# A two-layer decode kernel: one key/value head instead of two with stationary output weights, and an up projection with stationary weights

## The chip, the cores and the metric

The kernel runs on one core of one Trainium2 chip. The metric is the device time of one execution in microseconds (us), as the median of several runs. Lower is better. The profile is of one execution, taken by the hardware profiler.

## What is computed

One token for each of four requests passes twice through the same pair of blocks, attention with cached keys and values and then a gated feed-forward block:

```python
x = A_x
x = x + _A_ref(_layernorm(x), A_k_cache, A_v_cache, A_wq, A_wo)
x = x + _B_ref(_layernorm(x), B_w_gate, B_w_up, B_w_down)
x = x + _A_ref(_layernorm(x), A_k_cache, A_v_cache, A_wq, A_wo)
x = x + _B_ref(_layernorm(x), B_w_gate, B_w_up, B_w_down)

# _A_ref: q = x @ wq; softmax(q k^T / sqrt(128)) v over 4096 cached positions; @ wo
# _B_ref: (gelu(x @ w_gate) * (x @ w_up)) @ w_down
```

D is 512, there are 32 query heads and 8 key/value heads of 128, so that four query heads (rep) share a key/value head, and the feed-forward width is 1792. Keys and values of one request are 8 MB each; all of the cache is 67 MB in bfloat16.

## The kernel before

The kernel does not go block by block over all requests. For each request b it finishes the first attention and the first feed-forward block, and then uses the keys of that request that are still in SBUF for the second attention, while the keys of request b + 1 take their place. So the keys are read once, the values nearly twice (two tiles of a pass are kept).

**The stages.** `attend(None, 0)` (L495) is the first attention of request 0, with the loading of all weights. Then the loop at L662 runs over b = 0 to 3: `dense` (L643) finishes the first layer of request b for one row, queries for its second attention are built, and `attend(b, b + 1)` does the second attention of b and the first of b + 1 together. For b = 3 `attend_last` (L603) does the second attention alone. One more `dense` call for all four rows, and the output is written.

**Values in steps.** A key/value head of values comes in two tiles of 512 KB. `Values.step` (L466) does one such tile: 16 matmuls with a block of values as the stationary operand and four columns of probabilities as the moving one, into `ot`. A pass of one request over its values has 16 steps. Seven buffers hold value tiles; after a step the buffer is free and `load_v` (L453) issues the next load from the SP queue. After every four steps, which are two key/value heads, one VectorE instruction (L487) multiplies `ot` with the reciprocal of the softmax sum and writes eight columns of `OT_bf` (first attention) or `OT2_bf` (second). The last 14 steps of the second attention's pass are spread over the following dense stage and the start of the next `attend`: `fill` (L663) and `rest` are calls of its `step`. So between the matmuls of the dense stage there are value steps.

**The output projection.** `pairs` (L492) gives the first query head of each of the four groups of eight heads, in the order in which the values finish. Three groups go through `out_proj` (L275), "the rows": each head's column of `OT_bf` is stationary and the 512 columns of its `wo` rows move; the four heads of a key/value head go to four strips of 32 partitions of a PSUM tile `rows`. When the three groups are in, `y_rows` (L259) turns `rows` in 32x32 blocks on VectorE (L215) and copies it (L261), and `y_select` (L264) adds the four strips up with 8 small matmuls into `y`. The fourth group, which finishes last, goes through `out_proj_end` (L283): blocks of `wo` are stationary, 4 for each head, and a head's column moves. That adds into `y` and needs no turn. So 8 heads are 32 matmuls there.

**The dense stage** calls in this order: `out_proj_end`, fill(1), the addition to x (`add_y`, L290) and the layernorm sums, fill(1), the gate projection `ffn_in` (L300) with `wg_sb`, fill(1), the up projection with `wu_sb`, `gelu`, `gate_up`, fill(2), `down` (L344) and a second `add_y`. For one row (nb = 1) `ffn_in` keeps the row stationary and moves the weights, 64 matmuls of 448 columns, into `rows`; `ffn_cols` (L319) then turns the rows with one VectorE instruction. For four rows it keeps 128x128 weight blocks stationary and moves the rows, 56 matmuls, and no turn follows.

**Order.** The order of instructions on each engine is the order of the program. The places that matter below: in `attend`, L594 to L601, the last five value steps of the pass with the third group of heads, `y_rows` and `y_select` between them; in `attend_last`, L629 to L641, the same for four rows; in `attend`, L513 to L523, `rest(1)`, the second group's scores, `soft`, `rest(1)`, `soft_turn` (L408, a VectorE turn of `pp`, L410), `soft_swap`, `rest(2)`.

Of the kernel before, what the change touches and what calls it, by code (L numbers as in the profile page):

```python
# [30 lines left out]
def kernel(  # L31
# [240 lines left out]
    def head_rhs(o_bf, i):  # L272
        return o_bf[:, i:i + 1] if len(o_bf.shape) == 2 else o_bf[:, i, :]

    def out_proj(rows, o_bf, h0, hp, at):  # L275
        for n in range(hp):
            i = h0 + n
            lhsT = head_rhs(o_bf, i)
            r0 = (i % QD) * QS
            nc.tensor.matmul(rows[r0:r0 + lhsT.shape[-1], :], lhsT=lhsT, rhs=wo_sb[:, i, :],  # L280
                             start=(at == 0 and n < QD), stop=(at == 2 and n >= hp - QD))

    def out_proj_end(y, o_bf, h0, hp):  # L283
        for k in range(KD):
# [12 lines left out]
            nc.vector.tensor_tensor(out=XX[:, 0, bs], in0=XX[:, 0, bs],  # L297
                                    in1=y.rearrange("p k b -> p b k"), op=ALU.add)

    def ffn_in(b0, nb, w_sb):  # L300
        bs = slice(b0, b0 + nb)
        rows = new_rows()
        if nb > 1:
            h = rows[:, :KF * nb].rearrange("p (c j) -> p c j", j=nb)
            for c in range(KF):
                for k in range(KD):
                    nc.tensor.matmul(h[:, c], lhsT=w_sb[:, k, c * P:(c + 1) * P],
                                     rhs=xn_bf[:, k, bs], start=(c == 0 and k == 0),
                                     stop=(k == KD - 1), skip_group_check=True)
            return h  # L310
        for k in range(KD):
            w = w_sb[:, k].rearrange("p (n a i) -> p a n i", a=QD, i=QS)
            for j in range(QD):
                nc.tensor.matmul(rows[j * QS:j * QS + nb, :KF * QS], lhsT=xn_bf[:, k, bs],  # L314
                                 rhs=w[:, j], start=(k == 0), stop=(k == KD - 1))
        return rows

    def ffn_cols(h, nb):
        return h if nb > 1 else turn_rows(h, KF * QS)[:, :, :nb]  # L319

    def gelu(nb, rows, rstd):
        hg = ffn_cols(rows, nb)
# [139 lines left out]
    class Values:  # L462
# [3 lines left out]
        def step(self, count=1):  # L466
            for _ in range(count):
                use = self.order[self.n]
                assert order[seen["use"]] == use
                seen["use"] += 1  # L470
                b, last, g, s, t = use
                pe, rden = self.prob[g]
                if self.n % (2 * NT) == 0:
                    self.ot = ps_ot.tile([P, 2, rep], FP32, name="ot", tag="ot")
                self.n += 1
                load_v()
                v = held[b, g, s, t]
                for i in range(CH):
                    c = t * CH + i
                    nc.tensor.matmul(self.ot[:, s % 2], lhsT=v[:, i, :], rhs=pe[:, s, c, :],  # L480
                                     start=(c == 0), stop=(c == C - 1), skip_group_check=True)
                if last or (b, g, s, t) not in keep:
                    free.append(held.pop((b, g, s, t)))
                load_v()
                if self.n % (2 * NT) == 0:
                    s0 = s - s % 2
                    nc.vector.tensor_tensor(  # L487
                        out=self.dst(g * GH + s0).rearrange("p (k h) -> p k h", h=rep),
                        in0=self.ot[:], in1=rden[:, s0:s0 + 2], op=ALU.mult)


    def pairs(order):  # L492
        return [(order[n][2] * GH + order[n][3] // 2 * 2) * rep for n in range(0, VB, 2 * NT)]

    def attend(b2, b1, next_q=None, rest=None):  # L495
        two, first = b2 is not None, b1 == 0
# [1 line left out]
        ga, gb = groups(b1)  # L498
        keys = Keys(b1)
        turn = keys.turn  # L500
        vals = Values(b1, 0, prob1, lambda k: OT_bf[:, k * rep:(k + 2) * rep])
        vals2 = None
        if two:
            vals2 = Values(b2, 1, prob2, lambda k: OT2_bf[:, k * rep:(k + 2) * rep, b2])
            sc2 = [new_scores(i) for i in range(NG)]
            seen["hold"] = True
            scores(sc2[0], ga, 0)
            keys.load(GH)
            qm1 = next_q()
            scores(sc2[0], ga, 1)  # L510
            keys.load(GH)
            q_build(qm1, gb)
            rest(1)  # L513
            for t in range(NT):
                scores(sc2[1], gb, t)
                keys.load(GH)
            seen["hold"] = False
            load_v()
            p0 = soft(sc2[0])
            rest(1)  # L520
            soft_turn(p0)
            pe0, den0 = soft_swap(p0, p2p), soft_den(p0)
            rest(2)  # L523
            qm = q_spread(q1_bf[:, ga, :, b1], amask, ga)
            turn()
            prob2[ga] = (pe0, soft_recip(den0))
            q_build(qm, ga)
            vals2.step(KEEP)
            turn(3)
        else:  # L530
            load_wq(0)
            keys.load(TG)
            load_wq(1)
            keys.load(TG)
            load_v()
            make_identity(nc, ident_bf[:])
            build_consts()
            xT_ps = ps_sm.tile([P, KD, B], BF16, name="xT_ps", tag="sm")
            for k in range(KD):
                nc.tensor.transpose(xT_ps[:, k, :], x_bf[:B, k * P:(k + 1) * P], ident_bf[:B, :B])  # L540
            nc.vector.tensor_copy(out=XX[:, 0].rearrange("p b k -> p k b"), in_=xT_ps[:])
            ln_square(0, B)
            rstd1 = ln_rstd(B, ln_center(0, B))
            q_first(q_rows(0, B, 0), 0, rstd1)
            build_q1(0, 0)
            turn(4)
# [26 lines left out]
        soft_turn(p0)  # L573
        if not first:
            for i in range(2):
                out_proj(rows, OT_bf, heads[i], hp, i)
        pe, den = soft_swap(p0, p1p), soft_den(p0)
        if two:
            p1 = soft(sc2[1])
# [6 lines left out]
        if first:  # L586
# [2 lines left out]
            seen["upto"] = len(loads)  # L589
            load_v()  # L590
            for i in range(3):
                out_proj(rows, OT_bf, heads[i], hp, i)
            y = y_select(y_rows(rows, 1), 1)
        else:  # L594
            vals.step(2)
            out_proj(rows, OT_bf, heads[2], hp, 2)
            yc = y_rows(rows, 1)
            vals.step()
            y = y_select(yc, 1)
            vals.step(2)  # L600
        return (y, OT_bf, heads[3], hp), vals2  # L601

    def attend_last(b2, next_q, rest):  # L603
        prob2 = {}
        ga, gb = groups(b2 + 1)
        vals = Values(b2, 1, prob2, lambda k: OT2_bf[:, k * rep:(k + 2) * rep, b2])
        sc2 = [new_scores(i) for i in range(NG)]
        def freed(t):
            scores(sc2[0], ga, t)
# [19 lines left out]
        vals.step(4)  # L629
        soft_turn(p0)  # L630
        prob2[gb] = (soft_swap(p0, p2p), soft_recip(soft_den(p0)))
        out_proj(rows, OT2_bf, heads[0], hp, 0)
        vals.step(5)
        out_proj(rows, OT2_bf, heads[1], hp, 1)
        vals.step(4)
        out_proj(rows, OT2_bf, heads[2], hp, 2)
        yc = y_rows(rows, B)
        vals.step(2)
        y = y_select(yc, B)
        vals.step()  # L640
        return y, OT2_bf, heads[3], hp  # L641

    def dense(b0, nb, proj, fill):  # L643
        out_proj_end(*proj)
# [3 lines left out]
        ln_square(b0, nb)  # L648
        mv = ln_center(b0, nb)
        fill(1)  # L650
        rg = ffn_in(b0, nb, wg_sb)
        fill(1)
        ru = ffn_in(b0, nb, wu_sb)
        sq, h = gelu(nb, rg, ln_rstd(nb, mv))
        H_bf = gate_up(nb, sq, h, ru)
        fill(2)
# [71 lines left out]
```

## Time and profile before

| What | us |
|---|---|
| median of 7 runs | 314.33 |
| lowest and highest | 313.27 and 316.86 |
| the profiled execution, device time | 314.11 |
| its span, first to last instruction | 312.3 |
| TensorE matmuls (PE) busy | 211.7 (68%) |
| TensorE weight loads (PEld) busy, beside matmuls | 123.2 (39%) |
| VectorE (DVE) busy | 169.9 (54%) |
| ScalarE (ACT) busy | 29.0 (9%) |
| read from HBM | 110.37 MB, 353 GB/s over the span |

The span leaves out 1.8 us of the profiled execution's own time. The mean granted TensorE clock is 0.696 of full speed; after the first 98 us it is 0.50 but for four short bursts of 1.00.

The groups of the profile that belong to the parts concerned are these: `out_proj` for one row, 96 matmuls of 615 ns each by the record (four run side by side); `out_proj_end` for one row, 128 matmuls of 165 ns each, pipelined; the up projection for one row, 64 matmuls of 567 ns; the turns of gate and up rows, 8 of 662 ns; the turns of 512 columns, 15 of 729 ns; the evictions of `ot`, 32 of 170 ns.

A timeline line has the start in us, the duration in us (of all its instructions together), engine, line, operation, output and inputs, shapes and the number of instructions. In brackets stands how long the engine was idle before it and what ended that.

### The profile page before, as it was taken

How to read it: one execution, taken by the hardware profiler on the slowest of the kernel's cores; microseconds unless marked ns; L12 is line 12 of the kernel's file. 1: busy time of each engine (PE TensorE's matmuls, PEld its weight loads, DVE VectorE, ACT ScalarE, POOL GpSimd, SP SyncE). 2: the span in 40 equal slices, each digit the busy share in tenths (PEclk: the TensorE clock that was granted, in tenths of full speed). 3: DMA queues.
4: the chain of work that ended last, by engine and by line, in shares of the span. 5: the costliest groups of instructions: out<-in, count | busy, mean ns of one | idle time of the engine just before them, and what ended most of it. 6: DMA issues, size and time to landing. Idle time of an engine off the chain costs nothing.

```text
span 312.3 us, 8784 instructions
## 1 busy us (share of the span) xinstructions
PE 211.7 (68%) x3892; PEld 123.2 (39%) x3892; DVE 169.9 (54%) x473; ACT 29.0 (9%) x70; POOL 0.7 (0%) x6
## 2 busy tenths in 40 slices
PE   1360585243676657899966389899662898997875
PEld 0110255111323134657441246664412466646554
DVE  5585751014348895445378954464789544544033
ACT  0003001000002021200010203000102030004000
POOL 0000000000000000000000000000000000000000
PEclk9999999999997555555775555577655555568555
DMA  6999999999959999999999999999999999999910
GB/s 257 383 412 394 408 411 406 355 371 392 384 164 353 409 408 340 315 370 284 384 409 409 409 409 397 359 311 372 410 408 409 408 407 391 315 324 393 406 60 3
DMA packets 34662, 110.94 MB, mean 355 GB/s; under 512 B 3128, under 2 KB 9024, under 8 KB 34624
## 3 DMA queue, kind: packets, MB, share of 16 engines
q1 hardware_dynamic: 34624, 110.38, 93.4%
q8 instruction: 30, 0.49, 0.7%
q14 instruction: 8, 0.07, 0.1%
HBM read 110.37 MB, written 0.00 MB: 353 GB/s over the span
## 4 chain that ended last, share of the span: by engine, by line
DMA 48%; PE 24%; DVE 14%; SPq 9%; issue 2%; ACT 1%; DVEq 0%; ACTq 0%
DMA kt<-in_A_k_cache_dram 22%; DMA v<-in_A_v_cache_dram 20%; PE sc L383 6%; PE ot L480 5%; DVE kt L372 5%; DMA kt<-in_A_v_cache_dram 3%; PE rows L314 3%; DMA wd_sb<-in_B_w_down_dram 3%; SPq L127 3%; SPq L133 3%; PE rows L280 2%; PE rows L225 2%; PE y L347 2%; DVE rows L215 1%; PE x L429 1%
## 5 line engine op out<-in xcount | busy, mean ns | idle before, releaser
L480 PEld LDWEIGHTS <-v 128*128 128x128 bf16 x1920 | 60.2, 104 | 47.9 <-issue 24.0
L480 PE MATMUL ot<-pe,v 128*128 128x4 bf16 x1920 | 64.0, 166 | 19.3 <-DMA v<-in_A_v_cache_dram 16.0
L372 DVE STREAM_TRANSPOSE kt<-kt 128x1024 f32<-128x1024 f32 x64 | 74.1, 1210 | 4.1 <-DMA kt<-in_A_k_cache_dram 4.1
L383 PE MATMUL sc<-kt,qb 128*32 128x512 bf16 x512 | 63.7, 544 | 15.1 <-DVE kt L372 13.5
L215 DVE STREAM_TRANSPOSE rows<-rows 128x512 f32<-128x512 f32 (+1 forms) x23 | 16.2, 706 | 41.2 <-PE rows L225 19.1
L383 PEld LDWEIGHTS <-qb 128*32 128x32 bf16 x512 | 17.1, 115 | 45.9 <-issue 32.6
L402 ACT ACTIVATE pp<-sc,nm 128x512 bf16<-128x512 f32 x16 | 11.0, 688 | 153.9 <-DVE junk L398 153.8
L429 PE MATMUL x<-pp,ident_bf 128*32 128x128 bf16 x256 | 9.1, 283 | 22.1 <-DVE pp L410 22.0
L225 PE MATMUL rows<-wq_sb,xn_bf 128*1 128x512 bf16 (+1 forms) x160 | 18.2, 603 | 4.8 <-DMA wq_sb<-in_A_wq_dram 4.5
L487 DVE TENSOR_TENSOR OT_bf<-ot,rden 128x8 bf16<-128x8 f32 x32 | 5.5, 170 | 27.8 <-PE ot L480 26.8
L280 PE MATMUL rows<-wo_sb,OT_bf 128*1 128x512 bf16 (+1 forms) x120 | 14.8, 614 | 6.3 <-DMA wo_sb<-in_A_wo_dram 6.3
L389 DVE TENSOR_REDUCE m<-sc 128x1 f32<-128x512 f32 x16 | 10.8, 678 | 13.2 <-PE sc L383 13.2
L429 PEld LDWEIGHTS <-ident_bf 128*32 128x32 bf16 x256 | 6.7, 121 | 28.2 <-issue 26.1
L410 DVE STREAM_TRANSPOSE pp<-pp 128x512 bf16<-128x512 bf16 x16 | 11.3, 703 | 7.9 <-ACT pp L402 7.5
L432 ACT CAST pe<-x 128x512 bf16<-128x512 f32 x16 | 9.4, 586 | 18.6 <-PE x L429 18.6
L246 PE MATMUL qe<-qm,t_bf 128*128 128x64 bf16 x16 | 3.4, 215 | 10.7 <-DVE qm L236 6.6
L347 PE MATMUL y<-H_bf,wd_sb 128*128 128x1 bf16 (+1 forms) x280 | 8.4, 165 | 2.8 <-DVE H_bf L340 1.5
L249 DVE TENSOR_TENSOR qb<-qe,amask 128x256 bf16<-128x256 f32 x16 | 6.8, 424 | 5.4 <-PE qe L246 5.4
L225 PEld LDWEIGHTS <-xn_bf 128*1 128x1 bf16 (+1 forms) x160 | 4.5, 111 | 13.1 <-issue 12.0
L347 PEld LDWEIGHTS <-wd_sb 128*128 128x128 bf16 x280 | 8.0, 103 | 4.1 <-DMA wd_sb<-in_B_w_down_dram 3.0
L415 PE MATMUL den<-zx,mean_f 128*128 128x16 f32 x32 | 8.9, 357 | 0.0
L420 DVE RECIPROCAL rden<-den 128x16 f32<-128x16 f32 x16 | 4.0, 250 | 8.5 <-PE den L415 8.1
(78 smaller groups left out, 127.5 us busy)
## 6 DMA issues: line engine op xcount, KB each, us to landing
v<-in_A_v_cache_dram SPq DMA_DIRECT2D x112, 512.0 KB, 8.1
kt<-in_A_k_cache_dram SPq DMA_DIRECT2D x64, 512.0 KB, 10.2
wq_sb<-in_A_wq_dram SPq DMA_DIRECT2D x2, 2048.0 KB, 11.2
wo_sb<-in_A_wo_dram SPq DMA_DIRECT2D x4, 1024.0 KB, 11.8
kt<-in_A_v_cache_dram SPq DMA_DIRECT2D x8, 512.0 KB, 9.9
wg_sb<-in_B_w_gate_dram SPq DMA_DIRECT2D x1, 1792.0 KB, 13.5
wu_sb<-in_B_w_up_dram SPq DMA_DIRECT2D x1, 1792.0 KB
wd_sb<-in_B_w_down_dram SPq DMA_DIRECT2D x1, 896.0 KB, 15.9
```

What stands on the lines that cost most here:

```text
L215: nc.vector.transpose(out=rows[:, :n], in_=rows[:, :n])
L225: nc.tensor.matmul(rows[j * QS:j * QS + nb, :], lhsT=xn_bf[:, k, bs], rhs=w, start=(k == 0), stop=(k == KD - 1))
L280: nc.tensor.matmul(rows[r0:r0 + lhsT.shape[-1], :], lhsT=lhsT, rhs=wo_sb[:, i, :], start=(at == 0 and n < QD), stop=(at == 2 and n >= hp - ...
L347: nc.tensor.matmul(y[:, k], lhsT=wd_sb[:, c, k * P:(k + 1) * P], rhs=H_bf[:, c, :], start=(c == 0 and k == 0), stop=(c == KF - 1), skip_gr ...
L372: nc.vector.transpose(out=words, in_=words)
L383: nc.tensor.matmul(sc[s * QS:(s + 1) * QS], lhsT=qb[:, w0:w0 + 2 * W], rhs=kt[:, :, be // 2, :, be % 2], start=(t == 0 and be == 0), stop= ...
L389: nc.vector.tensor_reduce(out=m[:], in_=sc.rearrange("p c j -> p (c j)"), axis=AX.X, op=ALU.max)
L402: nc.scalar.activation(out=pp[:], in_=sc[:], func=ACT.Exp, bias=nm[:, 0:1], scale=scale, accum_out=ls[:])
L410: nc.vector.transpose(out=flat, in_=flat)
L429: nc.tensor.matmul(x[a * QS:(a + 1) * QS, s], lhsT=ident_bf[:, s * QS:(s + 1) * QS], rhs=pT[:, a], start=True, stop=True, skip_group_check ...
L432: nc.scalar.copy(out=pe.rearrange("p s c h -> p (s c h)"), in_=x.rearrange("p s t c h -> p (s t c h)"))
L480: nc.tensor.matmul(self.ot[:, s % 2], lhsT=v[:, i, :], rhs=pe[:, s, c, :], start=(c == 0), stop=(c == C - 1), skip_group_check=True)
```

## The change

Three things are changed.

1. Of the last group of eight heads in a pass, only the four query heads of the last key/value head still go through `out_proj_end`, 16 matmuls. The other four join the rows: a call of `out_proj` with four heads is put after step 14 of the pass, and `y_rows` comes after it; `y_select` moves behind step 15. This holds for `attend` of requests 1 to 3 and for `attend_last`. The first `attend` keeps groups of eight.
2. So that these four heads are there early, the last two key/value heads of every pass are evicted from `ot` one by one, after steps 14 and 16, in place of once after step 16. This holds for every pass over values, the first and the second attention of each request.
3. The up projection of one row is done like that of four rows: 56 matmuls with stationary weight blocks, and no turn. The gate projection of one row is left as it was.

The diff, cut to what is spoken of:

```diff
-    def out_proj(rows, o_bf, h0, hp, at):
+    def out_proj(rows, o_bf, h0, hp, start=False, stop=False):
...
-                             start=(at == 0 and n < QD), stop=(at == 2 and n >= hp - QD))
+                             start=(start and n < QD), stop=(stop and n >= hp - QD))
...
-    def ffn_in(b0, nb, w_sb):
+    def ffn_in(b0, nb, w_sb, cols):
         bs = slice(b0, b0 + nb)
         rows = new_rows()
-        if nb > 1:
+        if cols:
...
     def ffn_cols(h, nb):
-        return h if nb > 1 else turn_rows(h, KF * QS)[:, :, :nb]
+        return h[0] if h[1] else turn_rows(h[0], KF * QS)[:, :, :nb]
...
-                if self.n % (2 * NT) == 0:
-                    s0 = s - s % 2
+                m = 1 if self.n > VB - 2 * NT else 2
+                if self.n % (m * NT) == 0:
+                    s0 = s // m * m
                     nc.vector.tensor_tensor(
-                        out=self.dst(g * GH + s0).rearrange("p (k h) -> p k h", h=rep),
-                        in0=self.ot[:], in1=rden[:, s0:s0 + 2], op=ALU.mult)
+                        out=self.dst(g * GH + s0, m).rearrange("p (k h) -> p k h", h=rep),
+                        in0=self.ot[:, s0 % 2:s0 % 2 + m], in1=rden[:, s0:s0 + m], op=ALU.mult)
...
     def pairs(order):
-        return [(order[n][2] * GH + order[n][3] // 2 * 2) * rep for n in range(0, VB, 2 * NT)]
+        at = [(u[2] * GH + u[3]) * rep for u in order]
+        return [at[n] // (2 * rep) * 2 * rep for n in range(0, VB, 2 * NT)] + [at[-3], at[-1]]
...
-        else:
-            vals.step(2)
-            out_proj(rows, OT_bf, heads[2], hp, 2)
-            yc = y_rows(rows, 1)
-            vals.step()
-            y = y_select(yc, 1)
-            vals.step(2)
-        return (y, OT_bf, heads[3], hp), vals2
+            return (y, OT_bf, heads[3], hp), vals2
+        vals.step(2)
+        out_proj(rows, OT_bf, heads[2], hp)
+        vals.step()
+        out_proj(rows, OT_bf, heads[4], rep, False, True)
+        yc = y_rows(rows, 1)
+        vals.step()
+        y = y_select(yc, 1)
+        vals.step()
+        return (y, OT_bf, heads[5], rep), vals2
...
-        out_proj(rows, OT2_bf, heads[2], hp, 2)
+        out_proj(rows, OT2_bf, heads[2], hp)
+        vals.step()
+        out_proj(rows, OT2_bf, heads[4], rep, False, True)
         yc = y_rows(rows, B)
-        vals.step(2)
+        vals.step()
         y = y_select(yc, B)
         vals.step()
-        return y, OT2_bf, heads[3], hp
+        return y, OT2_bf, heads[5], rep
...
-        rg = ffn_in(b0, nb, wg_sb)
+        rg = ffn_in(b0, nb, wg_sb, nb > 1)
         fill(1)
-        ru = ffn_in(b0, nb, wu_sb)
+        ru = ffn_in(b0, nb, wu_sb, True)
```

## The prediction

> **What bounds the kernel now.** I read the slices of the page first, then the table of stages (busy time, granted clock, DMA rate), then the chain of waits inside the poor stages, then the timeline there.
>
> ```profile
> DMA  6999999999959999999999999999999999999910
> GB/s 257 383 412 394 408 411 406 355 371 392 384 164 353 409 408 340 315 370 284 384 409 409 409 409 397 359 311 372 410 408 409 408 407 391 315 324 393 406 60 3
> q1 hardware_dynamic: 34624, 110.38, 93.4%
> 152.00:193.00 41.00, 28.49 (x494) 15.86 (x486) 29.58 (x54) 6.59 (x16) 0.00 (x0) 0.58 1.03 409
> 200.00:215.00 15.00, 14.35 (x280) 7.99 (x281) 8.04 (x43) 0.21 (x1) 0.00 (x0) 0.63 0.95 336
> 215.00:256.00 41.00, 28.11 (x495) 15.86 (x488) 29.84 (x55) 6.59 (x16) 0.00 (x0) 0.58 1.03 409
> 264.00:281.00 17.00, 16.23 (x304) 9.09 (x304) 9.00 (x39) 0.21 (x1) 0.00 (x0) 0.55 0.94 321
> 300.00:312.30 12.30, 7.35 (x222) 6.68 (x218) 4.49 (x24) 0.25 (x1) 0.00 (x0) 0.50 0.01 2
> ```
>
> (In a stage line: stretch, us, then busy PE, PEld, DVE, ACT, POOL, then clock, DMA share, GB/s.) The 111 MB are read at 409 GB/s through both attention stretches: there DMA is the bound and a small delay costs nothing. The rate falls to 320 to 350 in the dense stages of requests 1, 2 and 3 (about 128 to 152, 193 to 215, 256 to 281), because a value buffer comes free only as the TensorE reaches the next value step between the dense matmuls. There, and in the last 12.3 us with no DMA at all, the PE/DVE chain is the bound, and a microsecond of it is a microsecond. Request 0's dense stage is different: it waits for its weights.
>
> The end of attention before a dense stage, request 2, from the timeline:
>
> ```profile
> 193.94 1.02 PE L280 MATMUL rows<-wo_sb,OT_bf 128*1 128x512 bf16 x8
> 194.90 0.59 PE L480 MATMUL ot<-pe,v 128*128 128x4 bf16 x16
> 195.02 0.73 DVE L215 STREAM_TRANSPOSE rows<-rows 128x512 f32<-128x512 f32 x1 [1.62 <-PE rows L280]
> 196.01 0.29 PE L268 MATMUL y<-yc,s_f 128*32 128x4 f32 x8 [0.53 <-DVE yc L261]
> 196.23 1.21 PE L480 MATMUL ot<-pe,v 128*128 128x4 bf16 x32
> 197.70 0.99 PE L286 MATMUL y<-OT_bf,wo_sb 128*128 128x1 bf16 x32 [0.26 <-DVE OT_bf L487]
> 198.56 0.57 PE L480 MATMUL ot<-pe,v 128*128 128x4 bf16 x16
> ```
>
> Already one value step (194.90) is too short to cover the turn of rows: PE idles 0.53. And the end of the up projection, request 1:
>
> ```profile
> 138.96 1.66 PE L314 MATMUL rows<-wu_sb,xn_bf 128*1 128x448 bf16 x16
> 140.56 1.01 PE L480 MATMUL ot<-pe,v 128*128 128x4 bf16 x32
> 140.68 0.67 DVE L215 STREAM_TRANSPOSE rows<-rows 128x448 f32<-128x448 f32 x1 [0.34 <-PE rows L314]
> 141.67 1.66 PE L347 MATMUL y<-H_bf,wd_sb 128*128 128x1 bf16 x56
> ```
>
> The 0.67 us turn of up lies almost wholly beside the two value steps that fill issues there.
>
> [...] down's 56 one-column matmuls start at 141.67, the next step at 143.19, so 27 ns each. [...] the 16 matmuls of up (567 ns each by their row) hold the PE 1.60 us, four at a time. [...]
>
> **The change part by part.** All dense stages that matter ran at clock 0.50.
>
> *End of attention, requests 1 to 3* (three times). Count from the start of step 14 (194.90 in request 2). New order: step 14, its eviction, 4 row matmuls, turn, copy, step 15 beside them, y_select, step 16, eviction, 16 matmuls. Step 14 ends at 0.59; the eviction starts 0.03 later and PE goes on 0.22 after that (197.48 to 197.70): 0.84. The 4 row matmuls are half of 8, which hold PE 0.95: 0.48, with results at 0.84 + 0.60 = 1.44. Turn from 1.50, 0.73; copy from 2.26; y_select 0.23 after the copy's start, 2.49, for 0.22; step 16 from 2.71 to 3.30; eviction and its latency 0.25; 16 matmuls from 3.55, half of the 0.84 that 32 hold PE: 0.42. The first fill step then starts at 3.97. Before it was 198.56 - 194.90 = 3.66 here, 134.99 - 131.53 = 3.46 in request 1, 261.07 - 257.36 = 3.71 in request 3. So the path grows by 0.31, 0.51 and 0.26: the second half of the rows comes a whole eviction later, and the 16 matmuls taken away (0.42) do not pay for the added eviction wait, row matmuls and the longer wait for the turn. In request 1 the step at 136.33 waits 0.17 for a value load anyway: 0.34 counts. Sum +0.91.
>
> *Up with stationary weights, requests 1 to 3.* 64 row matmuls become 56 one-column ones: 1.60 becomes 1.52 (down's row), -0.08. The turn goes (-0.67 of DVE), but what is late next is PE itself: two value steps of 0.47 end at 141.50, and down starts there instead of 141.67. H_bf is ready by then: up's last result at about 140.6, H_bf 0.17. So -0.17, -0.19 (204.99 to 204.80), -0.17 (267.50 to 267.33). With the three -0.08: -0.77.
>
> *Request 2's load.* The chain goes from the step at 203.94 through a load issued at 204.49 that takes 6.27 us to the step at 211.22. That issue comes 0.31 - 0.08 later, and PE's own slack there is only 0.19, so the -0.19 of this stage is mostly not collected: +0.2.
>
> *Request 0.* No value steps run there, so the turn of up is bare, but down's last 12 matmuls wait for wd_sb to land at 82.9, while H_bf was ready at 80.4. Gain 0. In the first attention pass the split eviction may stop PE once for 0.25 between steps 14 and 15; the wo_sb load that PE then waits for (up to 65.7) hides it.
>
> *Tail.* Step 14 of the last pass starts at 297.50. By the same count, with the 0.23 copy of four requests in place of 0.17, step 16 starts at 297.50 + 2.71 + 0.1 = 300.33, not when its load lands (299.81): +0.52. After it 16 matmuls fewer: -0.42. Sum +0.10.
>
> *Split evictions elsewhere.* Eight more evictions of 0.17. The one that matters is in the second pass over values: step 14 sits behind 32 score matmuls, and its eviction is now queued on DVE ahead of the turn of pp (L410), which holds the softmax. In request 2: step 218.74 to 219.30, eviction to 219.5, turn at 219.53 instead of 218.94: 0.6 later, in requests 1 to 3. Behind it wait the x matmuls, pe, two value steps, the turns of keys. I cost it at 0, because DMA covers it: in request 1 the PE then sits 2.69 us waiting for a value load (179.01), in the last request 0.7 (294.75). If that cover were gone it would be 3 x 0.6 = 1.8. Below nothing it cannot be. The SP queue has its last loads placed 10 us before they land, so a slot freed 0.6 later starves nothing.
>
> *Clock.* Up gives the array one moving column instead of 448. The only warm burst inside a dense stage (204.5 to 207.8) began after such a block; losing it would cost about 0.3 (st 0.56 for 0.35, down 1.66 for 1.55). One profile does not show whether it would go: 0 to 0.3, I take 0.
>
> Sum: +0.91 - 0.77 + 0.2 + 0.10 = +0.4. The profiled execution took 314.11 for a span of 312.3; 312.7 + 1.8 = 314.5. It lies 0.2 under the median of 314.33, so 314.7 for a median.
>
> **The rivals.** *Slower:* the eviction queued ahead of the turn of pp is not covered: the later softmax frees value slots late enough that loads slip in each of three passes. It decides once the delay passes the 0.7 us of waiting in the last pass. For it: DVE is 100% busy for 9 us afterwards. Against: 409 GB/s there. Price 1.8 with the +0.4: 316.5. *Faster:* the removals come out in full: 0.67 + 0.42 in three stages and 0.42 in the tail, 3.7 us, 310.6; half of it 312.5. For it: the chain of waits passes through the 32 matmuls in requests 2 and 3. Against: the fill steps and the idle PE before y_select. *Clock:* the +0.4 plus lost warm bursts, 315.0 to 315.5.
>
> **How the numbers follow.** About 0.5% (1.6 us) is what a measurement tells from no change. Likeliest case 0.55, with the clock case 0.08 beside it, nearly all within 0.5%; slower rival 0.26, mostly beyond; faster 0.11, mostly beyond. The range 313.0 to 316.6 takes in the likeliest, its clock bound and the slower rival's price, and leaves out the faster one. Likeliest case alone: 313.7 to 315.5.
>
> **What would show it.** Right: step 14 to the first fill step near 4.0 us in three places, PE idle about 0.6 before y_select; up about 1.52 and down directly after the two value steps; step 16 of the last pass at about 0.5 after its load; 409 GB/s unchanged in the attention stretches. Wrong: the rate there falls after the delayed turn, or the fill step comes at 3.5 or earlier.

## The result and the profile after

The changed kernel took 318.23 us in the median (315.87 to 321.42, 15 runs), the kernel before 314.95 beside it (312.26 to 318.55, 36 runs): a ratio of 1.010, 95% interval 1.0072 to 1.0128. Two later comparisons gave 1.0082 (1.0053 to 1.0111) and 1.0081 (1.0049 to 1.0114). So the change costs about 2.6 to 3.1 us, where +0.4 was forecast. Ratios leave out executions that lie more than 1.5% above the fastest of their kernel, which takes less out of a version with few runs: by the medians of all runs, two versions described further down would be lower, `gate_cols` (6 runs each time) at 1.0084 and 1.0062 and `front256` at 1.0008.

The changed kernel was profiled three times, in executions of 321.42, 319.56 and 318.01 us; the lines below are from the second, which is about 1 us slower than the median. First the rate in 40 slices of its span and the instruction queue, from its page:

```profile
GB/s 260 382 411 400 406 410 402 350 380 382 390 137 394 385 408 284 358 348 269 348 409 410 408 408 407 390 320 266 404 408 408 409 343 349 302 370 360 412 73 3
q8 instruction: 31, 0.51, 0.7%
```

Then the table by stretch (us, busy PE, PEld, DVE, ACT, POOL, clock, DMA share, GB/s), with the stretches moved to where the stages now lie:

```profile
152.00:193.00 41.00, 29.13 (x489) 15.47 (x485) 29.36 (x54) 6.04 (x15) 0.00 (x0) 0.58 1.02 398
193.00:216.00 23.00, 19.19 (x455) 13.71 (x447) 9.61 (x52) 0.80 (x2) 0.00 (x0) 0.50 0.96 359
216.00:257.00 41.00, 28.17 (x437) 14.08 (x430) 28.50 (x52) 4.71 (x12) 0.00 (x0) 0.58 0.99 382
257.00:282.00 25.00, 21.65 (x508) 15.67 (x512) 10.61 (x54) 2.09 (x6) 0.00 (x0) 0.50 0.96 333
305.30:317.80 12.50, 7.34 (x214) 6.64 (x214) 4.59 (x25) 0.25 (x1) 0.00 (x0) 0.50 0.01 3
```

The reader is to see two things. The tail without DMA is as long as before: the last value load lands at 305.21, 12.58 us ahead of the end, and in the kernel before at 299.77, 12.56 ahead. So in this pair of profiles all of the loss lies before the last load has landed: somewhere the stream of loads was starved. And TensorE has fewer busy microseconds in the dense stretch (19.19 of 23.00 for 455 matmuls) than in the kernel before:

```profile
193.00:215.00 22.00, 20.14 (x425) 12.58 (x425) 9.85 (x52) 0.21 (x1) 0.00 (x0) 0.59 0.96 341
```

So it stood idle there for 3.8 us instead of 1.9.

For what it waits, the timeline of request 1's dense stage, TensorE alone:

```profile
139.88 1.63 PE L307 MATMUL rows<-xn_bf,wu_sb 128*128 128x1 bf16 x56
141.37 0.99 PE L480 MATMUL ot<-pe,v 128*128 128x4 bf16 x32
142.22 1.42 PE L347 MATMUL y<-H_bf,wd_sb 128*128 128x1 bf16 x48
144.80 0.35 PE L347 MATMUL y<-H_bf,wd_sb 128*128 128x1 bf16 x8 [1.16 <-issue]
```

and two lines from request 2's:

```profile
211.67 1.01 PE L480 MATMUL ot<-pe,v 128*128 128x4 bf16 x32
214.38 0.23 PE L246 MATMUL qe<-qm,t_bf 128*128 128x64 bf16 x1 [1.69 <-issue]
```

Down starts right behind the value steps, 4.39 us after the gate's start instead of 4.82, as the change wants it. But in the middle of its 56 equal matmuls TensorE stands still for 1.16 us, and no semaphore explains it ("issue": it waited for nothing that the profile shows). Had down waited for `H_bf`, which one VectorE instruction writes whole, it would have waited ahead of its first matmul; the weights have lain in SBUF since request 0. No stall of this kind stands in the profile before.

**Where these stalls lie.** Counting TensorE's instructions (each matmul is two, a weight load and a matmul: 4004 of each on the page), every such stall stands, by the trace's count, at the 193rd of a group of 256. The queue q8 above carries 31 instruction packets, 0.51 MB together, each of 16,384 bytes in the trace, one for about 256 instructions (8,035 in the trace). The packets are put beside the boundaries in this table, worked out from the second profile of the changed kernel (all times in us; first the number of the boundary's instruction and the time at which TensorE passed it, then the packet that holds what comes next, as inferred from the order in time, and the stall):

```
boundary  passed   previous boundary   256 took   packet starts  ends     stall
2753      144.80   140.09              4.71       142.00         143.41   1.2
4545      207.03   201.78              5.24       204.49         205.55   0.5
4801      214.37   207.03              7.35       212.09         213.11   1.7
7105      292.61   286.40              6.21       290.33         291.30   0.6
7361      298.80   292.61              6.19       296.37         297.44   0.3
```

The packet with the next instructions starts only after TensorE has passed the boundary before, 1.9 to 5.1 us after it here; it takes 1.0 to 1.4 us, and TensorE goes on 1.3 to 1.5 us after its end. That is 4.7 to 7.4 us for 256 instructions at these five places, while the loads run, and the five stalls come to 4.3 us. The changed kernel can use them faster: up (56 pairs), two value steps (32) and down (56) follow one another at about 27 ns a pair (up's 56 start at 139.88 and the next step at 141.37), and 128 pairs are 256 instructions in 3.4 us. Before, up's 16 long matmuls held TensorE 1.60 us within that run.

### The profile page after: what moved, and what is told of

Same layout as the page of the kernel before. It is cut to its first block, busy times and chain, and to the rows that moved or that the text cites. A ratio compares the mean times of both kernels' runs of the same rounds, so it can differ in the third digit from the quotient of the medians.

```text
span 319.6 us, 9015 instructions
## 1 busy us (share of the span) xinstructions
PE 213.6 (67%) x4004; PEld 127.0 (40%) x4004; DVE 168.9 (53%) x477; ACT 29.0 (9%) x70; POOL 0.7 (0%) x6
## 4 chain that ended last, share of the span: by engine, by line
PE 35%; DMA 29%; DVE 22%; SPq 8%; issue 3%; ACT 1%; DVEq 0%; ACTq 0%
DMA v<-in_A_v_cache_dram 17%; DVE kt L372 11%; PE ot L480 10%; PE sc L383 9%; DMA kt<-in_A_k_cache_dram 9%; PE rows L280 4%; DMA wd_sb<-in_B_w_down_dram 3%; SPq L127 3%; SPq L133 3%; PE x L429 2%; PE rows L225 2%; DVE pp L410 2%; PE rows L314 1%; PE rows L307 1%; DVE qb L249 1%
## 5 line engine op out<-in xcount | busy, mean ns | idle before, releaser
L383 PE MATMUL sc<-kt,qb 128*32 128x512 bf16 x512 | 64.5, 552 | 15.3 <-DVE kt L372 13.8
L215 DVE STREAM_TRANSPOSE rows<-rows 128x512 f32<-128x512 f32 (+1 forms) x19 | 13.6, 715 | 33.5 <-PE rows L225 19.6
L488 DVE TENSOR_TENSOR OT_bf<-ot,rden 128x8 bf16<-128x8 f32 (+1 forms) x40 | 6.7, 168 | 39.1 <-PE ot L480 38.4
L280 PE MATMUL rows<-wo_sb,OT_bf 128*1 128x512 bf16 (+1 forms) x136 | 17.2, 611 | 7.4 <-DMA wo_sb<-in_A_wo_dram 6.3
L225 PE MATMUL rows<-wq_sb,xn_bf 128*1 128x512 bf16 (+1 forms) x160 | 18.9, 623 | 4.7 <-DMA wq_sb<-in_A_wq_dram 4.4
L389 DVE TENSOR_REDUCE m<-sc 128x1 f32<-128x512 f32 x16 | 10.8, 678 | 13.3 <-PE sc L383 13.3
L307 PE MATMUL rows<-xn_bf,wu_sb 128*128 128x1 bf16 (+1 forms) x280 | 8.2, 165 | 2.9 <-DMA wu_sb<-in_B_w_up_dram 2.9
L293 DVE SCALAR_TENSOR_TENSOR XX<-XX,y 128x4 f32<-128x4 f32 x8 | 1.3, 158 | 15.6 <-PE y L347 11.6
```

Source lines behind the costliest of these rows:

```text
L215: nc.vector.transpose(out=rows[:, :n], in_=rows[:, :n])
L225: nc.tensor.matmul(rows[j * QS:j * QS + nb, :], lhsT=xn_bf[:, k, bs], rhs=w, start=(k == 0), stop=(k == KD - 1))
L383: nc.tensor.matmul(sc[s * QS:(s + 1) * QS], lhsT=qb[:, w0:w0 + 2 * W], rhs=kt[:, :, be // 2, :, be % 2], start=(t == 0 and be == 0), stop= ...
L389: nc.vector.tensor_reduce(out=m[:], in_=sc.rearrange("p c j -> p (c j)"), axis=AX.X, op=ALU.max)
```

## The experiments

Stalls below are the sum, in one profiled execution, of the waits at such boundaries, each from the start of the instruction ahead of it to the start of the one behind, short ones included (so 5.1 here for the 4.3 of idle time above); ratios are to the kernel before on the same chip, with 95% intervals. Added matmuls have one column, and their result isn't used.

```
kernel                                          stalls us      ratio
changed (three profiles)                        3.6 5.1 2.9    1.0100  1.0082  1.0081
up_only                                         1.6            1.0022  0.9996 to 1.0047
heads_only                                      0              1.0001  0.9969 to 1.0033
split_only                                      0              1.0011  0.9983 to 1.0039
changed +256 instructions (twice)               2.9 1.6        1.0035  1.0012 to 1.0057
                                                               1.0016  0.9977 to 1.0055
changed +256, earlier place (front256)          4.3            1.0052  1.0027 to 1.0078
changed +512                                    1.9            1.0040  1.0010 to 1.0069
changed +144                                    3.1            1.0051  1.0021 to 1.0082
changed +64                                     2.8            1.0091  1.0059 to 1.0123
heads_only +64                                  0              1.0044  1.0014 to 1.0074
before +256                                     0              1.0004  0.9968 to 1.0040
gate for up in stationary weights (twice)       1.5 1.7        1.0113  1.0071 to 1.0154
                                                               1.0112  1.0073 to 1.0151
gate and up in stationary weights               4.9            1.0135  1.0089 to 1.0180
before + 12 long matmuls a dense stage          0              1.0091  1.0065 to 1.0118
before + 40 short matmuls a dense stage         2.3            1.0083  1.0055 to 1.0110
```

All fourteen profiles of versions with more short matmuls in the dense stages have such stalls, 1.5 us or more in sum; the six of versions without them, the kernel before among these, have none.

**One part alone.** `up_only` is the kernel before with only the new `ffn_in` and its calls; `split_only` has only the new evictions of `Values`; `heads_only` is the changed kernel without up:

```diff
-        ru = ffn_in(b0, nb, wu_sb, True)
+        ru = ffn_in(b0, nb, wu_sb, nb > 1)
```

> The kernel before, with the up projection alone changed (56 matmuls with stationary weights per dense stage in place of 16 with moving weights, no turn). Theory A, instruction supply: the 40 extra matmuls and weight loads per stage make the stretch up, two value steps, down so dense in instructions that the 16 KB instruction packets come too late behind the value loads; PE idles in the middle of a run of matmuls with no semaphore behind it. It expects most of the loss here, 316.5 to 318 against 315. Theory B, the end of attention and the evictions: this edit alone gains what the prediction's up term says, 0.25 in each of three stages, so 314 to 315.

> The changed kernel with the up projection as before (rows and turn). What remains is one head group of four in the rows, and the split evictions. Theory A (instruction supply) expects 315 to 316: the path at the end of attention grows by 0.3 to 0.5 in three places, and 12 matmuls fewer per stage are on PE. Theory B (end of attention, evictions queued ahead of the turn of pp) expects the whole loss here, 317.5 to 318.5.

> The kernel before, with the last two heads of every pass evicted one by one and nothing else changed. It isolates the eviction that waits on VectorE ahead of the turn of pp. If that wait is covered by DMA, as the prediction had it, 315 within 0.5; if it is the rival's 1.8, about 316.8, with the turn of pp 0.6 later in requests 1 to 3.

> The changed kernel again, for a second profile beside the others on the same chip: 318 by the result so far (ratio 1.01). Theory A expects gaps of about 1 us on PE without a semaphore, at other places perhaps than in the first profile[...]; theory B expects the same places to be late in both profiles, the turn of pp and the first fill step.

Each part alone costs nothing that can be told from no change, and 0.0022 and 0.0001 don't add up to 0.0082 on the same chip. So neither expectation held as put; the loss is in the two together. In the trace `up_only` has one long stall, in request 3's value step behind down:

```profile
271.84 0.35 PE L480 MATMUL ot<-pe,v 128*128 128x4 bf16 x8
273.46 0.35 PE L480 MATMUL ot<-pe,v 128*128 128x4 bf16 x8 [1.27 <-issue]
```

`heads_only` and `split_only` have none. The theory made from this: what costs is not the work but where TensorE's instruction boundaries fall in it, and the attention's new end, with 96 instructions fewer in the trace (7,716 in `heads_only`, 7,812 before), moves them.

**Shifting the program.** Instructions added where TensorE idles 7.6 us in the first attention move every later boundary by their number and leave the later work alone:

```diff
         scores(sc1, ga, 1)
+        if first:
+            pad = ps_sm.tile([P, 4], FP32, name="pad", tag="sm")
+            for _p in range(128):
+                nc.tensor.matmul(pad[:, :1], lhsT=ident_bf[:, :], rhs=ident_bf[:, :1],
+                                 start=True, stop=True)
```

(72 and 32 in place of 128 for 144 and 64 instructions.)

> The changed kernel with 128 one-column matmuls added in the first attention, right after the scores of sc1's second half, where TensorE has about 7 us to spare; their result is not used. They are 256 TensorE instructions (weight load and matmul each). Theory of the instruction lines (TensorE fetches its program in pieces of 256 instructions, and the stalls fall where a piece is used up in less time than the next takes to come): a shift by a whole piece leaves every later boundary at the same place in the work, so the time is the changed kernel's, 1.006 to 1.011 of before, with stalls at the same instructions of the dense stages as without the addition (down and the gates' neighbours). Rival (the loss is from how the value buffers and transfers fall together): also the changed kernel's time, 1.006 to 1.011. This run is the control for the next two: it says what the added matmuls cost by themselves, which both put at 0 to 0.5 us.

> The changed kernel with 72 of the same one-column matmuls at the same place, 144 TensorE instructions; their result is not used. Theory of the instruction lines: the boundaries now fall so that more of the pieces lie over the fast stretch of up, two value steps and down; adding up what each piece lacks against 5.2 us gives 6.0 us where the changed kernel has 3.0, so the time is 1 to 3 us above the control, 1.011 to 1.019 of before. Rival (value buffers and transfers): as the control within 0.5 us, 1.006 to 1.011 of before.

> The changed kernel with 32 of the same one-column matmuls at the same place, 64 TensorE instructions; their result is not used. Theory of the instruction lines: the sum of what the pieces lack is 2.5 us, near the changed kernel's 3.0, the least that any shift gives it, so the time is 0 to 0.8 us below the control, 1.004 to 1.010 of before, and the stalls stand at other instructions than in the control. Rival: as the control within 0.5 us, and whatever stalls there are stand at the same instructions.

> The kernel with the change of the attention's end and of the value steps but up as before, with 32 of the same one-column matmuls at the same place, 64 TensorE instructions; their result is not used. Unpadded it took 1.000 of before. Theory of the instruction lines: the shift moves boundaries onto the denser stretch (what the pieces lack goes from 0 to 2.2 us), so it is 0.5 to 2 us slower than unpadded, 1.002 to 1.007 of before, with stalls that wait for nothing in the dense stages. Rival (only the work itself counts): 1.000 within 0.002, no such stalls.

The stalls moved with the boundaries: the kernel padded by 256 has them again in down of request 1 and in the last values; the ones padded by 144 and 64 have them elsewhere. The sizes failed; they had been worked out with one time for every piece, 5.2 us, where the table above shows 4.7 to 7.4. The shift that should have been the worst (144) came out at 1.0051 and the one expected near the best (64) at 1.0091; the control, said to equal the changed kernel, took 0.005 of the loss back; and `heads_pad64` came out at 1.0044 with no stall at all. One stall of the run with 144 falls where nothing takes it back, with every load already issued:

```profile
298.98 0.43 PE L480 MATMUL ot<-pe,v 128*128 128x4 bf16 x11
301.00 0.70 PE L480 MATMUL ot<-pe,v 128*128 128x4 bf16 x21 [1.59 <-issue]
```

There the price of one is read off: from the last load's landing to the end it is 14.40 us in this execution, 12.4 to 12.6 in sixteen of the other profiles.

**Gate in place of up, and both.** `gate_cols` has the same number of short instructions, less tightly packed, and `both_cols` has more of them:

```diff
-        rg = ffn_in(b0, nb, wg_sb, nb > 1)
+        rg = ffn_in(b0, nb, wg_sb, True)
-        ru = ffn_in(b0, nb, wu_sb, True)
+        ru = ffn_in(b0, nb, wu_sb, nb > 1)
```

(`both_cols` has the first pair of lines only.)

> The changed kernel with the two projections of the dense stages exchanged: the gate takes stationary weights in all stages (56 short matmuls) and up goes back to the rows for one request (16 long ones). The number and kind of TensorE's instructions are the changed kernel's; only the fast runs no longer follow each other (gate, one value step, up as rows, two value steps, down), so 256 of them take 4.6 us or more instead of 3.4. Theory of the instruction lines: no stall that waits for nothing in the three dense stages, and the time comes back to 0.998 to 1.004 of before. Rival (80 more TensorE instructions a stage cost by themselves, or the attention's new end costs once up has no turn): as the changed kernel, 1.006 to 1.011.

> The changed kernel with the gate in stationary weights too: gate 56, value step 16, up 56, two value steps 32, down 56 pairs of weight load and matmul in one fast run, 432 instructions in about 6 us. Theory of the instruction lines: at least one boundary lies inside the run in every dense stage, and the piece behind it is short by 1 to 3 us: stalls of 1 to 3 us in each of the three stages, time 1.010 to 1.020 of before. Rival (only the work counts): the gate's turn is gone as well, so 0.2 to 0.5 us a stage below the changed kernel, 1.002 to 1.008, and no longer stalls than before.

> The changed kernel once more, beside the kernel with 256 added instructions on one chip. Both theories: 1.006 to 1.011 of before. If it is within 0.003 of the padded one here, the difference between 1.008 and 1.0035 in separate sets was the spread between sets; if it stays 0.004 above, the added matmuls did something more than shift the program.

> The changed kernel with 128 one-column matmuls added in the first attention, once more, beside the unpadded one; their result is not used. Theory of the instruction lines: equal to the changed kernel within 0.003, so 1.005 to 1.010. If the added matmuls did more than shift (they delay the first value steps and so the order of the loads): again 0.004 below the changed kernel, 1.002 to 1.005.

`both_cols` is the slowest of all, with stalls in requests 2 and 3 up to 2.0 us long; request 1's dense stage had none of note, where a long one had been expected in each. `gate_cols` went against the theory: 1.0113 and 1.0112. It has a stall in the gate of request 1:

```profile
137.76 1.20 PE L307 MATMUL rows<-xn_bf,wg_sb 128*128 128x1 bf16 x40
140.35 0.58 PE L307 MATMUL rows<-xn_bf,wg_sb 128*128 128x1 bf16 x16 [1.38 <-issue]
151.19 0.59 PE L480 MATMUL ot<-pe,v 128*128 128x4 bf16 x16 [0.71 <-DMA v<-in_A_v_cache_dram]
```

The packet there started 4.32 us after the boundary before was passed. With such a delay, and the 2.3 to 2.8 us from a packet's start to TensorE's going on in the table above, a piece that takes 5 us is too fast as well; the claim that only the run of up, values and down is too dense was too narrow. The last line shows the other way to lose: a value load that comes late, for which TensorE waits 0.71 us. On the same chip the changed kernel (1.0081) and the padded one (1.0016) again lay apart, 318.15 and 316.13 us in the median, so what the shift gives back is not the spread between sets. On the chip of the other shifts, the kernels padded by 256 and by 64 lay 2.0 us apart in the median.

**Which property of the shift.** The same matmuls put ahead of the first projection of the queries (`front256`), in both places (`pad512`), and into the kernel before:

```diff
+            pad = ps_sm.tile([P, 4], FP32, name="pad", tag="sm")
+            for _p in range(128):
+                nc.tensor.matmul(pad[:, :1], lhsT=ident_bf[:, :], rhs=ident_bf[:, :1],
+                                 start=True, stop=True)
             q_first(q_rows(0, B, 0), 0, rstd1)
```

> The changed kernel with the 128 one-column matmuls (256 TensorE instructions, result not used) put before the first projection of the queries instead, where TensorE waits for the first weights. If the shift of the program by one piece is what gave 0.6% back: 1.000 to 1.005 of before, and the stalls of the second dense stage absent as in the kernel padded later. If it was the place of the addition (what it does to the first attention): as the changed kernel, 1.006 to 1.011, with stalls in the second dense stage.

> The changed kernel with both additions, 512 TensorE instructions, result not used. If pieces alternate (every other one comes later), two pieces' shift is no shift: as the changed kernel, 1.006 to 1.011, with stalls in the second dense stage. If any whole number of pieces gives the same gain: 1.000 to 1.005. The plain theory of the boundaries, which said that a whole piece changes nothing, also puts it at 1.006 to 1.011.

> The kernel before with 128 one-column matmuls after the scores of sc1's second half in the first attention, result not used. If the addition helps by itself (it changes how the loads of the first attention fall, which carries on): 0.992 to 0.997 of before. If it acts only through the stalls, of which the kernel before has none: 0.998 to 1.002.

> The changed kernel with gate and up exchanged (gate with stationary weights, up in rows for one request), once more. Theory of the instruction lines as first put (only the fast run of up, values and down is too fast): 0.998 to 1.004. If any 80 further TensorE instructions in a dense stage cost, because each piece there is short of time: 1.005 to 1.012, as in the first run, with stalls in one or two dense stages.

For the kernel before, the addition can't be told from no change. In the changed kernel the ratio was lower with both places and both amounts, so neither the place nor an alternation of pieces looks like what matters; no unpadded changed kernel ran beside these two, though, and the interval of `front256` reaches 1.0078. `front256` kept its stalls in the second dense stage (1.0 and 1.3 us) and yet came out lower, so neither of its two expectations held. Packets come sooner or later by 2 us and more between executions: behind the boundary in request 2's down, the packet started after 4.1, 5.1 and 3.1 us in the three profiles of the changed kernel, after 3.0 and 0.5 in the two with 256 added, after 4.5 in `front256`. With 256 added in `pad256_again`, where it was 0.5 us, the DMA share was 0.93, so loads in flight don't settle it alone. What decides this delay was not found.

**Short or long, at the same place.** In the kernel before, in every dense stage of one request, 12 more long matmuls ahead of up, or 40 short ones behind it:

```diff
+        if w_sb is wu_sb:
+            for n in range(12):
+                nc.tensor.matmul(rows[n % QD * QS:n % QD * QS + nb, :KF * QS], lhsT=xn_bf[:, 0, bs],
+                                 rhs=w_sb[:, 0, :KF * QS], start=True, stop=True)
```

```diff
+        if w_sb is wu_sb:
+            for n in range(40):
+                nc.tensor.matmul(rows[n % QD * QS:n % QD * QS + nb, KF * QS:KF * QS + 1], lhsT=xn_bf[:, 0, bs],
+                                 rhs=w_sb[:, 0, :1], start=True, stop=True)
```

> The kernel before with 12 more row matmuls of 448 columns ahead of up in every dense stage of one request (24 TensorE instructions, about 1.2 us by up's own row; results overwritten). Both theories: no stall that waits for nothing; the dense stage is up to 1.2 us longer each time, of which the later waits for values may take a part: 1.002 to 1.011 of before.

> The kernel before with 40 one-column matmuls behind up in every dense stage of one request (80 TensorE instructions, about 1.1 us; results not used), so that 40, two value steps and down make 128 pairs, 256 instructions in 3.5 us, as up, value steps and down do in the changed kernel. Theory of the instruction pieces: stalls in one or more of the dense stages, 1 to 4 us in all, and 0.003 to 0.012 slower than the 12 long ones beside it. Rival (only TensorE's time counts, not the number of instructions): equal to the 12 long ones within 0.003 and no stalls.

The timelines of request 1's dense stage, first with the long ones:

```profile
139.31 1.21 PE L313 MATMUL rows<-wu_sb,xn_bf 128*1 128x448 bf16 x12
140.35 0.93 PE L318 MATMUL rows<-wu_sb,xn_bf 128*1 128x448 bf16 x16
141.21 0.96 PE L484 MATMUL ot<-pe,v 128*128 128x4 bf16 x32
142.32 1.55 PE L351 MATMUL y<-H_bf,wd_sb 128*128 128x1 bf16 x56 [0.16 <-DVE H_bf L344]
```

then with the short ones:

```profile
139.19 1.67 PE L314 MATMUL rows<-wu_sb,xn_bf 128*1 128x448 bf16 x16
140.63 0.48 PE L318 MATMUL rows<-wu_sb,xn_bf 128*1 128x1 bf16 x40
141.05 1.02 PE L484 MATMUL ot<-pe,v 128*128 128x4 bf16 x32
142.22 1.12 PE L351 MATMUL y<-H_bf,wd_sb 128*128 128x1 bf16 x36 [0.16 <-DVE H_bf L344]
144.49 0.70 PE L351 MATMUL y<-H_bf,wd_sb 128*128 128x1 bf16 x20 [1.14 <-issue]
```

From the gate's start (137.19 and 137.07) to down it is 5.13 and 5.15 us here, 0.3 over the 4.82 before. With the short ones it is 5.15 in all three stages. With the long ones it is 5.94 in requests 2 and 3, 1.12 over; in request 2:

```profile
202.09 1.29 PE L313 MATMUL rows<-wu_sb,xn_bf 128*1 128x448 bf16 x12
203.16 1.71 PE L318 MATMUL rows<-wu_sb,xn_bf 128*1 128x448 bf16 x16
205.91 1.55 PE L351 MATMUL y<-H_bf,wd_sb 128*128 128x1 bf16 x56
```

Up's own 16 matmuls took 0.86 us in request 1 and 1.64 here, because the granted clock (the third number from the end) was twice as high there:

```profile
140.35:142.30 1.95, 1.82 (x52) 1.14 (x44) 1.20 (x5) 0.22 (x1) 0.00 (x0) 1.00 0.94 321
203.16:204.80 1.64, 1.64 (x20) 0.41 (x12) 0.27 (x2) 0.21 (x1) 0.00 (x0) 0.50 0.92 347
```

So the long ones lengthen the three stages by 0.31, 1.12 and 1.12, 2.55 us together, near the 2.9 of their ratio, and bring no stall. The short ones lengthen them by 0.33 each, 1.0 together, and bring stalls: 1.1 us in down of request 1 and one in a value step of request 3, 2.3 from start to start. So many short instructions do cause the stalls, and TensorE's time alone doesn't, for the long ones take more of it. Both came out equally slow, 1.0091 and 1.0083, and the expectation of 0.003 to 0.012 between them failed: the long ones lose by their time nearly what the short ones lose by time and stalls.

**What this settles.** Shown: the stalls, their place at every 256th TensorE instruction after a late instruction packet, and that more short instructions in the dense stages bring them about. Shown too: much of the loss isn't the work as such, since the same work with 144 to 512 instructions added to it took 1.0016 to 1.0052 in all five such runs, two to four fifths less than 0.0088, the mean of the unpadded (with 64 added it took 1.0091). Only one of the five had the unpadded kernel beside it on its chip, at 1.0016 beside 1.0081.

That the stalls make up the whole loss is not shown. Take what the path from gate to down differs from 4.82 us over the three dense stages, where no stall falls into it, and add the stalls. That gives the changed kernel -1.3 + 3.9 = +2.6 us against 2.6 to 3.1 measured, `up_only` +0.3 against 0.7, the kernel padded by 256 +1.0 against 1.1 and 0.5, the one padded by 144 +1.8 against 1.6, by 512 +0.6 against 1.3, `both_cols` +3.6 against 4.3, the short matmuls +3.3 against 2.6, the long ones +2.55 against 2.9. But it gives `gate_cols` +1.2 against 3.6 (2.6 and 2.0 by the medians), `front256` +3.0 against 1.6, `heads_pad64` 0 against 1.4, and the one padded by 64 +1.5 against 2.9. The sums come from one to three executions, the ratios from 6 to 22, and the end of attention is left out of the sums, because `heads_only` shows no loss by it. Something besides may be at work, perhaps the stream of loads: in request 3's dense stage of `heads_pad64`, TensorE waits 0.46 us for a value load. That stays open. No version is shown to be faster than the kernel before.

## Why the prediction was wrong

*What bounds the kernel.* Right as far as it went: in the attention stretches DMA (409 GB/s before), in the dense stages TensorE's walk through the value steps that free the buffers. The landing of the last load plus 12.6 us is the span, before and in the second and third profile after (13.3 in the first). That all dense stages ran at clock 0.50 passes over request 2, for which the forecast's own table has 0.63.

*End of attention.* Right. From the group of 16 row matmuls to the layernorm's sums it took 12.06, 12.04 and 12.09 us before, and 12.57, 12.39 and 13.06 after; the last has a wait of 0.5 behind `y_select` in it that the first profile of the change (12.36) hasn't. That is +0.5, +0.3 and +0.3, as counted. The timeline shows the order foreseen, with step 14 at 196.02, the eviction's wait, four row matmuls, and 0.53 idle ahead of `y_select`:

```profile
196.02 0.59 PE L480 MATMUL ot<-pe,v 128*128 128x4 bf16 x16
196.86 0.60 PE L280 MATMUL rows<-wo_sb,OT_bf 128*1 128x512 bf16 x4 [0.25 <-DVE OT_bf L488]
197.39 0.58 PE L480 MATMUL ot<-pe,v 128*128 128x4 bf16 x16
198.50 0.29 PE L268 MATMUL y<-yc,s_f 128*32 128x4 f32 x8 [0.53 <-DVE yc L261]
198.72 0.59 PE L480 MATMUL ot<-pe,v 128*128 128x4 bf16 x16
199.56 0.57 PE L286 MATMUL y<-OT_bf,wo_sb 128*128 128x1 bf16 x16 [0.25 <-DVE OT_bf L488]
199.99 0.57 PE L480 MATMUL ot<-pe,v 128*128 128x4 bf16 x16
```

The fill step stands 3.97 us after step 14, the number of the forecast. What this path costs in the end was probably over-valued at 0.91: `heads_only`, with all of it, is at 1.0001, though its interval reaches 1.0 us. (By the forecast's own lines 32 matmuls hold TensorE 0.86 us, not 0.84; nothing hangs on it.)

*Up with stationary weights.* This is the step that failed. Its term, -0.77 us, knew only durations, and put the supply of TensorE's instructions at nothing without a word. The durations came out better than counted: the path gained 0.43 in each stage where no stall fell, -1.3 in all. But the stalls at late instruction packets came to 2.9 to 5.1 us in the three profiles, 3.9 in the mean, so that term and stalls are +2.6 together. The forecast took "64 row matmuls become 56", and the description ahead has 64 for one row too; the 64 are those of four stages, so a stage's 16 become 56, and with 40 matmuls come 40 weight loads. The 1.60 us was right, so this error isn't in a duration; what it hid is that TensorE has 80 more instructions to be fed in each dense stage. No case among the rivals had that. By itself the step costs little (`up_only`, 1.0022, with 1.6 us of stalls in its profile); the loss came out together with the attention's new end, which moves the boundaries.

*Split eviction ahead of the turn of pp.* The delay is there: from the first scores behind the dense stage to the x matmuls 9.0 us on average over the three requests in `split_only`, 8.4 before. Priced at nothing with a rival of 1.8 us (0.6%): `split_only` at 1.0011, with an upper bound of 1.0039, leaves that rival out for this part alone. In the changed kernel the rate in the attention stretches is 398 and 382 GB/s instead of 409, which the forecast named as a sign against itself; `split_only` shows 398 and 396 there without being slower.

*Request 2's load, request 0, the tail, the clock.* The tail's +0.10 measured +0.02. The granted clock of the dense stretches is 0.50 and the warm burst of request 2 is gone, but it is gone in `heads_only` too (0.50), which loses nothing. Request 2's +0.2 can't be told apart from the stalls there.

*Range and chances.* The slower rival had the right sign and a wrong mechanism. The measured time lies above the range because a cost of a kind that the profile before doesn't show had no place in it.

## What to carry to other kernels

Replacing few long matmuls by many short ones can cost even where TensorE's path gets shorter: here it fell by 0.43 us in a dense stage without a stall, and stalls of 2.9 to 5.1 us a profile came with it. Count instructions as well as microseconds, and ask how fast 256 of them are used up in the densest stretch: 3.4 us here, while at the stalls of one profile 256 took 4.7 to 7.4. A wait in the middle of a run of equal matmuls, put down to "issue" (1.16 us in down here), is a sign to look at the instruction packets. A control meant to lengthen a path by the same time has to be measured in every stage: the same 16 matmuls took 0.86 us in one at a granted clock of 1.00 and 1.64 in another at 0.50. And a result of under 1% that moves when unrelated instructions are added says little about the edit itself.

## What was not expected of the hardware

At the stalls of the changed kernel's second profile, a piece of 256 TensorE instructions took 4.7 to 7.4 us to arrive, counted from the passing of the boundary before, while loads ran at 269 to 412 GB/s in the slices of the page in which they lie; in the tail of the same profile, with DMA idle, the two packets start 0.5 and 0.3 us after the boundary. That the loads are what delays a packet is not shown: no run held them back. TensorE's 40 short matmuls with one stationary column, in four column strips, took 0.42 us, 10 ns each, where up's and down's one-column matmuls start 27 ns apart. Adding 256 instructions without a use made a kernel 0.65% faster on the same chip (1.0081 to 1.0016).
